# First product of the first MLP moved up to the transposes, and one attention unit started one tile later

## The chip, the cores and the metric

The kernel runs on one core of one Trainium2 chip. The metric is the device time of one execution in microseconds. Several executions of the same program are timed, and their median counts. One more execution is recorded by the hardware profiler; all rows below come from it.

## The reference

Three stages follow each other: a causal sparse attention, then two MLPs over its 2304 tokens.

```python
B, H, S, D = 4, 8, 576, 64
rel = pos[:, None] - pos[None, :]
mask_local   = (rel >= 0) & (rel < 32)                        # heads 0 to 3
mask_strided = (rel >= 0) & (pos[None, :] % 32 == pos[:, None] % 32)   # heads 4 to 7
attn = softmax(where(mask, q @ k.T / sqrt(D), -1e9)) @ v
x = attn.transpose(0, 2, 1, 3).reshape(2304, 512)             # tokens x (heads * D)
g = s * relu(x @ w_in) ** 2 + b                               # w_in 512 x 2048
y = g @ w_out                                                 # w_out 2048 x 512
out = ((y @ w_a) * (y @ w_b)) @ w_o2                          # w_a, w_b 512 x 1536
```

## The kernel before

**Numbers.** Every weight and activation that TensorE multiplies in the MLPs is split in two float32r halves, a high one made by ScalarE (ACT) and a low one made by VectorE (DVE) as source minus high. A product is then three matmuls, high by high, high by low, low by high (`PASSES`). The weights arrive as 64-bit floats; before the split each tile of 128 x 512 takes one ACT instruction (`raw`, a scaling) and three DVE instructions (a shift and two shift-and-or) to become float32.

**Blocks.** The first MLP runs over five token blocks. Block 0 holds the first 128 tokens of each of the four batches: 512 columns, of which the columns of batch bb are one quarter. Blocks 1 to 4 hold the rest of one batch each. A block is a loop over 16 tiles `f` of the 2048 hidden units. `h_mm(n, f)` makes one tile of h from x with 12 matmuls (four chunks `kk` of 128 of the 512 model dimensions, three passes each) into the one bank of the pool `ps_h`, then relu and square and the two halves of g. `o_mm` adds that tile's part of the output with 12 matmuls; it runs two tiles behind, so that the order of a tile is h(f), o(f-2), and then what `attend` issues.

**Opening.** x of block 0 comes from a dense little attention over the first 128 tokens of each batch (class `First`), whose order over all engines is written out in the string `ORDER`. Its last steps are `X` (TensorE transposes the result of one batch into a bank `fpx`), `hi` (ACT writes the high half of x for that batch's 128 columns and all four chunks `kk` at once) and `lo` (DVE writes the low half likewise). `I8` issues eight matmuls over constant data into a spare bank (`lull`). ACT's and DVE's instructions in `ORDER` are chained in that order.

**Attention beside the MLP.** x of block n+1 is made while the MLP of block n runs. A unit is a generator of steps for two heads: `local` for a window of 32 keys, `strided` for the strided heads. `plan(n)` puts each step behind a numbered tile, and `attend(number)` issues the steps of that tile, local units before strided ones. `in_order` makes every matmul of a step follow the last matmul issued before it, so TensorE's order is that of the code; within a step the planner may reorder matmuls that write different banks, but not those that add to one bank. ACT's and DVE's order is chosen by the planner when an instruction becomes ready; once queued, an instruction holds its place.

A local unit of block 1 has seven steps: (1) load q and k; (2) transpose them on TensorE (`pst`, two banks) and copy them by ACT into `qkT`; (3) load v, make the mask and the scores (`pss`, two banks), and DVE takes the row maximum; (4) four exponentials on ACT; (5) DVE normalises; (6) transpose the probabilities (`ppt`) and copy them by ACT into `pT`; (7) multiply with v (`po`) and write the halves of x. The first unit, u0, has its steps at (-5, -3, 0, 1, 1, 2, 3); a negative number is issued ahead of tile 0. The second, u1, has them at (1, 3, 4, 4, 5, 6, 7). The first strided unit, s0, has its transposes at 2 (three banks `pst`), its scores at 3 (two banks `pss`, into which no mask is multiplied: DVE adds it while it copies each bank out) and its exponentials at 4.

**Shared buffers.** The pool `ps_a` has three banks for all `pst`, `pss`, `ppt`, `po` of these units. `qkT` and `pT` of the local units share the one buffer of the tag `lT`. q and k of the local units share one buffer (`qk`), v another (`vn`). The exponentials of u0 are held behind the relu of the last tile of h issued before them.

Of the kernel before, what the change touches and what calls it, by code (L numbers as in the profile page):

```python
# [25 lines left out]
def sparse_attention_two_mlps(  # L26
# [21 lines left out]
    KD = DM // P  # L48
# [44 lines left out]
    def mm(*args, **kwargs):  # L93
        last_pe[:] = [nc.tensor.matmul(*args, **kwargs).ins]  # L94
# [15 lines left out]
    def split(hi, lo, src):  # L110
        nc.scalar.activation(out=hi, in_=src, func=AF.Copy)  # L111
        return nc.vector.tensor_tensor(out=lo, in0=src, in1=hi.bitcast(F32), op=ALU.subtract)  # L112
# [651 lines left out]
    def h_mm(n, f):  # L764
        T = T1[n]
        pool, tag = (ps_a, "a") if (n, f) == (0, 1) else (ps_h, "h")
        ph = pool.tile([P, TM], F32, tag=tag, name="h")[:, 0:T]
        m = 0
        for kk in (0, 2, 3, 1) if n and f == 0 else range(KD):
            for a, c in PASSES:  # L770
                mm(
                    ph, lhsT=wi[f][:, a, kk, :], rhs=x_t[n][:, c, kk, 0:T],
                    start=(m == 0), stop=(m == 3 * KD - 1),
                )
                m += 1
        with tc.high_priority(offset=URGENT):
            r = hp.tile([P, TM], F32, tag="r", name="r")[:, 0:T]
            relu = nc.scalar.activation(out=r, in_=ph, func=AF.Relu)  # L778
            gt = gp.tile([P, 2, TM], F32R, tag="gt", name="gt")
            hi, lo = gt[:, 0, 0:T], gt[:, 1, 0:T]  # L780
            if n == 0:
                nc.scalar.activation(out=r, in_=r, func=AF.Square)
                last = split(hi, lo, r)
            else:
                nc.scalar.activation(out=hi, in_=r, func=AF.Square)  # L785
                if n == 1:
                    nc.scalar.activation(out=gt[:, :, T:T + 2], in_=bc, func=AF.Copy)
                nc.vector.tensor_tensor(out=r, in0=r, in1=r, op=ALU.mult)  # L788
                last = nc.vector.tensor_tensor(out=lo, in0=r, in1=hi.bitcast(F32), op=ALU.subtract)  # L789
        behind[:] = [relu.ins, last.ins]  # L790
        return gt
# [212 lines left out]
    def plan(n):  # L1004
        at_n = (-2, 0, 1, 1, 2, 3, 4) if n == 1 else (-3, 0, 1, 2, 3, 4)
        at_f = (-3, 0, 1, 2, 4, 5) if n == 1 else (-3, 0, 1, 2, 3, 5)
        near = [
            (
                4 * i - 1,
                local(0, n, i % 2, TF + i // 2 * 4 * QT, 4 - i // 2) if n == 1  # L1010
                else local_pairs(n - 1, n, i % 2, TF + i // 2 * 8 * QS, 8 - i // 2 * 2),
                at_n,
            )
            for i in range(4)
        ]
        far = [(8 * i + 1, (strided if n == 1 else strided_pairs)(n - 1, n, i), at_f) for i in range(2)]
        if n == 1:
            near[0] = (0, near[0][1], (-5, -3, 0, 1, 1, 2, 3))
            far[0] = (1, far[0][1], (-5, 1, 2, 3, 5, 7))
        if n == 2:  # L1020
            near[0] = (-1, near[0][1], (-2, 0, 1, 2, 3, 4))
        for first_, gen, at in near + far:
            for t in at:
                steps.setdefault((n - 1) * NF1 + first_ + t, []).append(gen)
# [25 lines left out]
    def next_weights(number):  # L1050
# [13 lines left out]
    )  # L1064

    m_b = first_mask()
# [38 lines left out]
    for n in range(1, NB):  # L1105
        plan(n)
# [3 lines left out]
    for n in range(NB):  # L1110
# [11 lines left out]
        for f in range(NF1):  # L1122
            order = ExitStack()
            if n == 0:
                supply(len(wi) + len(wo) + 6)
                with after(behind + (last_w if f == 1 else []) or last_act + last_dve):
                    next_weights(min(1 if f == 0 else 2, len(order1) - len(wi) - len(wo)))
                order.enter_context(after(last_act + last_dve))
            gt = in_order(h_mm, n, f)
            queue.append((acc, gt, f, n))  # L1130
            if len(queue) > AHEAD1:
# [207 lines left out]
```

## Time and profile before

| what | value |
|---|---|
| time, median of 3 runs | 899.72 us (899.67 to 899.81) |
| the profiled execution's own time | 899.66 us |
| its span, first to last instruction | 897.6 us |
| TensorE matmuls (PE) busy | 888.7 us, 99% |
| TensorE weight loads (PEld) busy | 793.9 us, 88% |
| DVE busy | 621.8 us, 69% |
| ACT busy | 401.9 us, 45% |
| granted TensorE clock over the span | 1.000 |

The span is 2.06 us shorter than the time of the same execution. Matmuls are pipelined and their ends are modelled, so a PE that is busy 99% of the span is not yet one that never waits. A weight load (LDWEIGHTS) stands ahead of each matmul on the same engine, and a wait shows best as idle time ahead of a weight load: [0.95 <-ACT qkT L294] behind a row says that the engine stood idle for 0.95 us ahead of it, until that instruction of ACT released it.

### The profile page before, as it was taken

The numbers are of one execution on the slowest core, as the hardware profiler recorded it, in microseconds if no ns is written. First come the engines' busy times: TensorE is split into PE (matmuls) and PEld (weight loads), VectorE is DVE, ScalarE is ACT, GpSimd is POOL, SyncE is SP. The second block draws the span as 40 slices with busy tenths as digits, with TensorE's granted clock in tenths as the row PEclk, the third lists the DMA queues.
The fourth block names the chain that finished last, engine by engine and source line by source line (L and its number), as shares of the span: only waits on it lengthen the run. The fifth ranks groups of instructions, "written<-read, shape, count | busy, mean of one in ns | idle before, by whom it ended". The sixth has DMA issues, their size and how long they took to land.

```text
span 897.6 us, 16349 instructions
## 1 busy us (share of the span) xinstructions
PE 888.7 (99%) x6166; PEld 793.9 (88%) x6166; DVE 621.8 (69%) x1266; ACT 401.9 (45%) x866; POOL 42.0 (5%) x120
## 2 busy tenths in 40 slices
PE   8999999999999999999999999999999999999998
PEld 6778889999888899998889999988999988999986
DVE  6898995676766777727655777765676765776742
ACT  6777774434433353343333445444334444333322
POOL 6000000000000010000100000000000000000000
PEclk9999999999999999999999999999999999999999
DMA  9965534656665766446566443323432231333010
GB/s 232 283 209 161 166 78 133 164 143 166 201 168 163 178 190 169 133 130 225 195 198 225 131 141 112 131 87 108 148 99 98 89 94 59 124 95 106 30 36 35
DMA packets 156606, 126.41 MB, mean 141 GB/s; under 512 B 102256, under 2 KB 131440, under 8 KB 156528
## 3 DMA queue, kind: packets, MB, share of 16 engines
q1 hardware_dynamic: 149840, 109.12, 43.0%
q0 software_dynamic: 4608, 15.73, 4.5%
q8 instruction: 48, 0.79, 0.4%
q10 hardware_dynamic: 2080, 0.52, 0.3%
q14 instruction: 30, 0.25, 0.1%
HBM read 100.17 MB, written 25.17 MB: 140 GB/s over the span
## 4 chain that ended last, share of the span: by engine, by line
PE 96%; ACT 2%; DVE 1%; DMA 1%; issue 0%; SPq 0%; ACTq 0%
PE acc L94 38%; PE pp L94 29%; PE h L94 22%; PE po L94 2%; PE pss L94 1%; PE ppt L97 1%; PE fpo L94 1%; DMA fqk<-in_q_dram 1%; ACT raw L130 0%; ACT fpt L596 0%; PE fss L94 0%; PE fps L97 0%; PE pst L97 0%; PE fpp L97 0%; PE fpx L97 0%; ACT r L778 0%
## 5 line engine op out<-in xcount | busy, mean ns | idle before, releaser
L94 PE MATMUL pp<-x2w,wf 128*128 128x384 f32 x1512 | 265.8, 335 | 0.0
L94 PEld LDWEIGHTS pp<-x2w,wf 128*128 128x128 f32 x1512 | 263.0, 188 | 1.8 <-ACT u L596 0.4
L94 PE MATMUL h<-x,w 128*128 128x512 f32 (+1 forms) x960 | 217.1, 374 | 0.0
L94 PE MATMUL acc<-gt,w 128*128 128x512 f32 (+2 forms) x960 | 210.7, 368 | 1.0 <-ACT w L111 1.0
L94 PEld LDWEIGHTS acc<-gt,w 128*128 128x128 f32 x960 | 175.5, 188 | 24.0 <-ACT w L111 1.4
L94 PEld LDWEIGHTS h<-x,w 128*128 128x128 f32 x960 | 171.8, 188 | 24.3 <-DVE w L112 0.5
L94 PE MATMUL acc<-o2w,abt 128*128 128x512 f32 x648 | 150.5, 390 | 0.0
L94 PEld LDWEIGHTS acc<-o2w,abt 128*128 128x128 f32 x648 | 121.4, 188 | 24.6
L778 ACT ACTIVATE r<-h 128x512 f32<-128x512 f32 (+1 forms) x80 | 44.4, 555 | 156.3 <-PE h L94 152.6
L788 DVE TENSOR_TENSOR r<-r 128x384 f32<-128x384 f32 (+1 forms) x64 | 40.0, 625 | 91.8 <-ACT gt L785 91.6
L601 DVE TENSOR_TENSOR u<-pp,u 128x384 f32<-128x384 f32 x72 | 40.0, 555 | 64.8 <-PE pp L94 59.3
L596 ACT ACTIVATE u<-pp 128x384 f32<-128x384 f32 x36 | 17.8, 493 | 115.6 <-PE pp L94 115.6
L596 ACT ACTIVATE wf<-w2t 128x512 fp32r<-128x512 f32 x72 | 45.2, 628 | 21.2 <-PE pp L94 20.3
L601 DVE TENSOR_TENSOR wf<-w2t,wf 128x512 fp32r<-128x512 f32 x72 | 49.4, 686 | 0.3 <-ACT wf L596 0.3
L136 DVE SCALAR_TENSOR_TENSOR raw<-raw 128x512 uint32<-128x512 uint32 x66 | 44.4, 688 | 0.7
L130 ACT ACTIVATE raw<-raw 128x512 f32<-128x512 f32 x66 | 42.7, 672 | 2.9 <-DMA raw<-in_moe_w_a_dram 2.5
L789 DVE TENSOR_TENSOR gt<-r,gt 128x384 fp32r<-128x384 f32 (+1 forms) x64 | 40.0, 624 | 3.6
L601 DVE TENSOR_TENSOR wf<-w2r,wf 128x512 fp32r<-128x512 f32 x72 | 39.6, 550 | 0.0
L596 ACT ACTIVATE wf<-w2r 128x512 fp32r<-128x512 f32 x72 | 37.3, 518 | 4.5 <-PE pp L94 4.0
L601 DVE TENSOR_TENSOR abt<-dly,abt 128x384 fp32r<-128x384 f32 x36 | 19.9, 556 | 25.0 <-ACT abt L596 24.9
L596 ACT ACTIVATE abt<-c 128x384 fp32r<-128x384 f32 x36 | 18.8, 523 | 40.4 <-DVE c L601 40.4
L785 ACT ACTIVATE gt<-r 128x384 fp32r<-128x384 f32 (+1 forms) x64 | 36.5, 571 | 0.4
(150 smaller groups left out, 805.6 us busy)
## 6 DMA issues: line engine op xcount, KB each, us to landing
w2t<-w2s SPq DMA_DIRECT2D x36, 512.0 KB
w2r<-w2d SPq DMA_DIRECT2D x60, 256.0 KB
raw<-in_moe_w_out_dram SPq DMA_DIRECT2D x28, 512.0 KB
w2d<-w2s POOLq DMA_DIRECT2D x36, 256.0 KB, 3.3
raw<-in_moe_w_in_dram SPq DMA_DIRECT2D x16, 512.0 KB
raw<-in_moe_w_a_dram SPq DMA_DIRECT2D x12, 512.0 KB
raw<-in_moe_w_b_dram SPq DMA_DIRECT2D x12, 512.0 KB
w2s<-w2t POOLq DMA_DIRECT2D x12, 512.0 KB, 4.4
```

The lines of the kernel that those rows point to most:

```text
L94: last_pe[:] = [nc.tensor.matmul(*args, **kwargs).ins]
L97: last_pe[:] = [nc.tensor.transpose(*args).ins]
L130: nc.scalar.activation(out=high.bitcast(F32), in_=high.bitcast(F32), func=AF.Copy, scale=HIGH_SCALE)
L136: nc.vector.scalar_tensor_tensor(out=low, in0=high, scalar=3, in1=low, op0=ALU.logical_shift_left, op1=ALU.bitwise_or)
L596: i = nc.scalar.activation(**kwargs).ins
L601: i = getattr(nc.vector, method)(**kwargs).ins
L778: relu = nc.scalar.activation(out=r, in_=ph, func=AF.Relu)
L785: nc.scalar.activation(out=hi, in_=r, func=AF.Square)
L788: nc.vector.tensor_tensor(out=r, in0=r, in1=r, op=ALU.mult)
L789: last = nc.vector.tensor_tensor(out=lo, in0=r, in1=hi.bitcast(F32), op=ALU.subtract)
```

## The change

Three edits. `h_mm` takes the chunks of the first tile of block 0 in the order 0, 1, 3, 2. The steps (2) to (7) of u0 each move one tile later, step (2) from ahead of tile 0 to behind tile 0's h; its loads stay where they are. The eight `lull` matmuls behind the last `X` go, so that on TensorE the first h comes directly behind the transposes of x.

```diff
@@ h_mm @@
-        for kk in (0, 2, 3, 1) if n and f == 0 else range(KD):
+        for kk in range(KD) if f else (0, 2, 3, 1) if n else (0, 1, 3, 2):
             for a, c in PASSES:
                 mm(
                     ph, lhsT=wi[f][:, a, kk, :], rhs=x_t[n][:, c, kk, 0:T],
@@ plan @@
         if n == 1:
-            near[0] = (0, near[0][1], (-5, -3, 0, 1, 1, 2, 3))
+            near[0] = (0, near[0][1], (-5, 0, 1, 2, 2, 3, 4))
             far[0] = (1, far[0][1], (-5, 1, 2, 3, 5, 7))
@@ ORDER @@
-        "hi0 hi1 rc3 no2 no3 cl0 X3 lo0 lo1 hi3 X2 hi2 I8 lo3 lo2 d11 d21 ch1 cl1"
+        "hi0 hi1 rc3 no2 no3 cl0 X3 lo0 lo1 hi3 X2 hi2 lo3 lo2 d11 d21 ch1 cl1"
```

## Rows read from the trace of the kernel before

**Rows 1.** Busy time by stage (microseconds, instructions), then clock, DMA share, GB/s.

```profile
31.99:62.24 30.25, 28.32 (x200) 21.65 (x199) 27.85 (x55) 24.07 (x53) 0.00 (x0) 1.00 0.84 257
62.24:480.00 417.76, 417.76 (x3561) 362.37 (x3558) 295.87 (x648) 186.57 (x412) 27.42 (x50) 1.00 0.59 167
```

**Rows 2.** Timeline of the opening: start, microseconds, instruction, [idle before <-releaser].

```profile
2.92 2.74 PE L94 MATMUL lull<-ident_b 128*128 128x384 bf16 x8 [2.92 <-DVE ident_b L561]
...
28.70 2.08 ACT L596 ACTIVATE x<-fpx 128x512 fp32r<-128x512 f32 x4 [2.25 <-PE fpx L97]
...
29.46 2.48 DVE L601 TENSOR_TENSOR x<-fpx,x 128x512 fp32r<-128x512 f32 x4
29.79 1.03 SPq L298 DMA_DIRECT2D vn<-in_v_dram  x2
...
29.93 1.46 PE L94 MATMUL lull<-ident_b 128*128 128x384 bf16 x8
...
31.07 0.61 PEld L97 LDWEIGHTS pst<-ident,qk 128*128 128x128 f32 x5
...
31.64 0.69 ACT L294 ACTIVATE qkT<-pst 128x256 f32<-128x256 f32 x2 [0.87 <-PE pst L97]
...
31.99 2.38 PEld L94 LDWEIGHTS h<-x,w 128*128 128x128 f32 x11 [0.18 <-DVE x L601]
32.01 0.37 SPq L283 DMA_DIRECT2D qk<-in_q_dram  x1
```

**Rows 3.** Timeline of TensorE's weight loads, 33 to 63 us.

```profile
35.40 2.60 PEld L94 LDWEIGHTS h<-x,w 128*128 128x128 f32 x12
...
39.12 2.15 PEld L94 LDWEIGHTS h<-x,w 128*128 128x128 f32 x10 [0.47 <-DVE w L112]
42.72 2.61 PEld L94 LDWEIGHTS acc<-gt,w 128*128 128x128 f32 x12 [1.45 <-ACT w L111]
45.37 0.58 PEld L97 LDWEIGHTS ppt<-ident,lpt 128*96 128x96 f32 x4
...
47.22 2.60 PEld L94 LDWEIGHTS h<-x,w 128*128 128x128 f32 x12
49.85 2.68 PEld L94 LDWEIGHTS acc<-gt,w 128*128 128x128 f32 x12
52.88 0.55 PEld L94 LDWEIGHTS po<-pT,vn 96*64 96x64 f32 x16 [0.35 <-issue]
53.50 0.50 PEld L97 LDWEIGHTS pst<-ident,qk 128*128 128x128 f32 x5
54.95 0.88 PEld L94 LDWEIGHTS pss<-sqkT 64*64 64x64 f32 x32 [0.95 <-ACT qkT L294]
55.91 2.58 PEld L94 LDWEIGHTS h<-x,w 128*128 128x128 f32 x12
58.53 2.68 PEld L94 LDWEIGHTS acc<-gt,w 128*128 128x128 f32 x12
61.47 0.12 PEld L94 LDWEIGHTS <-ident_b 128*128 128x128 bf16 x2 [0.26 <-issue]
...
62.24 0.76 PEld L94 LDWEIGHTS h<-x,w 128*128 128x128 f32 x4
```

**Rows 4.** Timeline of ACT, 28 to 63 us.

```profile
39.05 0.34 ACT L237 ACTIVATE lpt<-pss,mx 128x96 f32<-128x96 f32 x1
...
40.32 1.28 ACT L130 ACTIVATE raw<-raw 128x512 f32<-128x512 f32 x2
...
41.97 0.69 ACT L111 ACTIVATE w<-raw 128x512 fp32r<-128x512 f32 x1
...
46.36 0.58 ACT L319 ACTIVATE pT<-ppt 96x512 f32<-96x512 f32 x1
```

**Rows 5.** Timeline of DVE, 28 to 63 us.

```profile
35.73 0.61 DVE L231 TENSOR_REDUCE mx<-pss 128x2 f32<-128x192 f32 x2
...
57.28 0.82 DVE L243 TENSOR_TENSOR spt<-pss,smask 128x288 f32<-128x288 f32 x2
```

## The prediction

> **What bounds the kernel now.** I read the busy times by stage first, since they say how far a delay travels. From 62.24 us to 480 us TensorE has a matmul under way in all of the 417.76 us, while from 31.99 to 62.24 it has one in 28.32 of 30.25 us [rows 1]. 62.24 is where h of tile 5 starts, the first work behind the last step that the change moves (u0's step 7, now behind tile 4). So I take what h(5) gains or loses as what the whole time gains or loses, and look only at the 30 us ahead of it.
>
> Next I read what opens that stretch. ACT's four high halves of x end at 28.70 + 2.08 = 30.78, DVE's four low halves at 29.46 + 2.48 = 31.94, and the weight load of h(0)'s second matmul starts at 31.99, named as released by DVE [rows 2]. DVE's last low half sets the start of h(0), not TensorE, which fills the time before with the eight `lull` matmuls and u0's transposes.
>
> Then the weight loads from 33 to 63 us, for the waits between the tiles [rows 3]. The reader is to see four. h(2) has its last ten loads at 39.12 though h(1)'s ended at 38.00: less two loads at 0.22 us each, 0.7 us of idling for weight halves. o(0) waits 1.45 us for ACT's half of its weights. At tile 3 the strided scores wait 0.95 us for ACT to empty u1's banks. At tile 4 there is only the 0.26 us that each such group of scores pays for issue. Between 31.99 and 62.24 DVE is busy 27.85 us and ACT 24.07 us [rows 1], so the weight halves of the first tiles are bound by these two, DVE before ACT.
>
> **The change part by part.**
>
> *Order of chunks, and the place of h(0).* Each `hi` and `lo` writes one batch's 128 columns of all four chunks; each product of h reads all 512 columns of one chunk. So any chunk needs all four quarters, and the order 0, 1, 3, 2 releases nothing. All twelve products add to one bank and keep their order; the second reads low halves. Only the first product can move, to about 30.85. The second still loads at 31.99, and h(0) ends its loads at 34.37 as before. The 1.46 us of `lull` and the 0.61 us of transposes that leave [rows 2] lay under DVE's low halves: gain 0. If that cover were not there, the most to be had would be 31.99 - 30.85 = 1.1 us.
>
> *The transposes behind h(0).* They now cost TensorE their 0.61 us in the open [rows 2], and the scores leave this place: those took 34.37 to 35.40, 1.03 us [rows 2, 3]. h(1) starts at 34.98, 0.4 us earlier, and ends its loads at 37.6. The scores behind it end at 38.6, inside the time in which h(2) waited for weights. So on TensorE both are free up to h(2).
>
> *ACT and DVE up to o(0).* u0's two copies took 0.69 us at 31.64, where ACT had idled 0.87 us [rows 2]. Now they stand behind h(0)'s relu, where ACT scales weights and makes the halves of g one after another, and DVE's next weights wait for those. Bounds 0 and 0.69; I take 0.69, for I see no idle time there. DVE's two row maxima, 0.61 us [rows 5], move from 35.73 to about 38.7, into the same chain: 0 to 0.61, I take 0.3. The other way, the exponentials leave ACT's queue ahead of o(0)'s weights, 39.05 to 40.32, 1.27 us; those weights come at 41.97 [rows 4]. That is worth 0 to 1.27; DVE being the fuller of the two, I take 0.3. Sum: o(0) at 42.72 + 0.7 = 43.4.
>
> *Tile 2.* u0's `ppt`, 0.58 us, leaves; s0's transposes, 45.95 to 47.22 = 1.27 us [rows 3], stay. They need three banks, two of which hold u0's scores until the exponentials, now behind h(2)'s relu, are done. o(0)'s 2.61 us covers most of that; uncovered 0 to 1.27, taken 0.2, since the scalings came only behind the exponentials (40.32 behind 39.05 [rows 4]) and so won't hold them up. h(3): 43.4 + 2.61 + 1.27 + 0.2 = 47.5, 0.3 late. ACT then carries the exponentials and not the 0.58 us copy of `pT` [rows 4], 0.69 us more, ahead of o(1)'s weights; o(1) followed h(3) at 49.85 without a wait [rows 3]. 0 to 0.69, taken 0.2. I stand at +0.5.
>
> *Tile 3.* Here the shared buffer tells. u0 now writes `pT` at this tile and reads it at the next; u1's copies into `qkT` want the same buffer `lT`, so they wait, and with them u1's two `pst` banks stay full. s0's two score banks must be had one after the other out of the third bank: `ppt` 0.58, its end 0.15, ACT's copy 0.58 and 0.2 until ACT is free, half of the scores' 0.88, DVE's mask add 0.41, the other 0.44, releases 0.2, all [rows 3 to 5] but the small ones. How long DVE lets the add wait: before, it came at 57.28 though the score loads ended at 55.83, 1.45 us later; nobody waited for it. 0 to 1.45, I take 0.7. Sum 3.7 us, against 52.53 to 55.91 = 3.38. I stand at +0.8; bounds of this tile -0.4 and +1.1.
>
> *Tile 4.* Before, 61.21 to 62.24, 1.03 us. Now u0's product with v, 0.35 + 0.55 [rows 3]; then u1's copies, 0.69 as at 31.64 [rows 2], with 0.1 to start and 0.2 for ACT to come free; then u1's scores, 0.77 without the issue gap. 2.66 us, +1.6; bounds +1.3 (ACT free at once) and +2.4 (a weight half and a half of x ahead of the copies, 0.69 and 0.39). Nothing else is on TensorE between, by the order of the code.
>
> *DMAs.* u0's loads of q and k stay. Its loads of v (1.03 us of SP's queue) come a tile later for a use a tile later. u1's q and k, first issued at 32.01 [rows 2], now wait for u0's transposes, to 35.0 in place of 31.7, with weight loads behind them on SP's queue. The use is at 53.50, and the weights run six tiles of 128 x 512 ahead: 0, for up to 3.3 us of waiting. POOL has no part.
>
> *Sum.* 0.7 + (0.3 - 0.7) + 0.2 + 0.3 + 1.6 = **+2.4 us**. The profiled execution took 899.66 us, 0.06 under the median, so 902.1 us. All low ends together give about -1, all high ends about +6.
>
> One queue matters for tile 4. Between h(1)'s relu and its square ACT ran four exponentials and two scalings, from 39.05 to 41.6 [rows 4]: what is queued goes first. [...]
>
> **The rivals.**
>
> *The exponentials give it back (not slower).* Place: ACT ahead of o(0). If ACT and not DVE set o(0)'s 41.97, the 1.27 us comes off in full and h(2)'s wait is already filled. Then o(0) is at 42.72 + 0.69 + 0.3 - 1.27 = 42.44, 1.0 us better than in my sum, and tiles 3 and 4 at their low ends take 1.0 less: 902.1 - 2.0 = 900.1 us. It decides if tiles 3 and 4 cost under 1.8 us more than o(0) gains. For it speaks o(0)'s wait, released by ACT [rows 3]; against it DVE's 27.85 of 30.25 us.
>
> *h(0) does go by quarters.* If products that need only high halves went first, eight would fit between 30.85 and 32.6, and h(0) would end 0.9 us earlier, and relu and all weights with it: 901.2 us. Against it: in [rows 2] the loads stop at the second product.
>
> *ACT is held up at tile 4.* The copies are queued ahead of h(4)'s relu or the halves for tile 5, and all of it waits for u0's product: 2 us more, 904.1 us. The planner queues what it takes to be ready, and its times are not the chip's.
>
> *The clock falls.* Without `lull`, TensorE has one product between 30.0 and 31.99. After the opening's idle 2.92 us eight such matmuls took 2.74 us, and 1.46 later [rows 2]. At that pace h(0) and h(1) would take 88% more, 2 x 2.6 x 0.88 = 4.6 us: 906.7. [...]
>
> **How the numbers follow.** Forecast 0.58, exponentials 0.22, quarters 0.05, ACT held up 0.12, clock 0.03. A measurement of this kernel tells 0.2%, 1.8 us, from no change. Of the forecast, a sixth lies under +1.8; of the exponentials' case nearly all lies within 1.8 us, some 0.03 below. Faster 0.03, same 0.31, slower 0.66. A tenth on either side leaves 900.0 to 904.6 us; the forecast's own range is 901.0 to 903.6.
>
> **What would show it.** Right: the load of h(0)'s second product still at about 32.0, idle TensorE before it, clock 1.00; u0's copies behind h(0)'s relu; o(0) at 43 to 44; the strided scores of tile 3 in two groups with a wait for DVE between; u1's scores at tile 4 waiting some 0.8 us or more for ACT `qkT`; h(5) at 64 to 65 and no waits after. Wrong: h(0) ending before 34, o(0) before 42.7, or u1's scores at tile 4 following `po` at once.

## The result, and the profile after

The changed kernel took 905.51 us (median of 6 runs, 903.60 to 906.78), the kernel before 899.74 in the same comparison (6 runs, 899.50 to 899.81): a ratio of 1.0064, 95% interval 1.0051 to 1.0077, so 5.8 us slower. 902.1 was forecast, with a range up to 904.6: the sign was right, the loss more than twice as large. The profiled execution took 905.85 us, with a span of 903.8 and a mean granted clock of 0.998 (before: 899.66, 897.6, 1.000). The runs of one kernel now differ by 3 us, where those of before differed by 0.3. Two single executions in the comparisons further down, one of 2257 us (order and lull alone) and one of 3107 us (the kernel before), are left out of every median and range.

Where the time went is read by setting equal weight loads of the two traces side by side:

| place | before | after | behind by |
|---|---|---|---|
| h(0), second product | 31.99 | 32.61 | 0.62 |
| h(5) | 62.24 | 65.30 | 3.06 |
| h behind `po` of block 1's tile 7 | 194.29 | 198.89 | 4.60 |
| the next h | 199.46 | 205.63 | 6.17 |
| span | 897.6 | 903.8 | 6.2 |

The first 0.62 us come before anything that the change touches (at 7.5 us a transpose waits 0.58 us for a load where it waited 0.29, and the transposes of x start 0.63 us late); over the kernels below it is anything from -0.1 to 0.6, so I take it off. What is left is 2.44 us up to h(5), nothing for 130 us, and then 3.1 us in a place where the change moves nothing.

The busy times by stage, as in [rows 1] (columns as there). The first row has 32.69 us where it had 30.25; in the second TensorE is no longer busy throughout: 1.37 us are idle.

```profile
32.61:65.30 32.69, 28.74 (x204) 22.63 (x204) 28.62 (x57) 25.59 (x54) 0.00 (x0) 1.00 0.73 225
65.30:480.00 414.70, 413.33 (x3533) 358.86 (x3530) 293.23 (x643) 183.16 (x407) 27.36 (x50) 1.00 0.60 166
```

The opening, against [rows 2]. DVE's four low halves of x end at 32.56, and the second product loads right behind them; ahead of it TensorE idles. That is as before, without the `lull`.

```profile
29.32 2.08 ACT L596 ACTIVATE x<-fpx 128x512 fp32r<-128x512 f32 x4 [2.25 <-PE fpx L97]
...
30.08 2.48 DVE L601 TENSOR_TENSOR x<-fpx,x 128x512 fp32r<-128x512 f32 x4
...
31.45 0.19 PEld L94 LDWEIGHTS h<-x,w 128*128 128x128 f32 x1 [0.98 <-ACT x L596]
```

TensorE's weight loads of the first tiles, against [rows 3]. h(2) no longer waits, o(0) waits longer, and the strided scores of tile 3 come in two groups of 16 with 1.50 us of DVE between them. At tile 4 `po` is followed by u1's scores only 1.70 us later.

```profile
32.61 2.40 PEld L94 LDWEIGHTS h<-x,w 128*128 128x128 f32 x11 [0.97 <-DVE x L601]
35.05 0.67 PEld L97 LDWEIGHTS pst<-ident,qk 128*128 128x128 f32 x5
...
39.29 2.61 PEld L94 LDWEIGHTS h<-x,w 128*128 128x128 f32 x12
44.12 2.61 PEld L94 LDWEIGHTS acc<-gt,w 128*128 128x128 f32 x12 [2.22 <-ACT w L111]
...
50.49 2.68 PEld L94 LDWEIGHTS acc<-gt,w 128*128 128x128 f32 x12
...
54.73 0.57 PEld L94 LDWEIGHTS pss<-sqkT 64*64 64x64 f32 x16 [0.40 <-ACT pT L319]
56.79 0.57 PEld L94 LDWEIGHTS pss<-sqkT 64*64 64x64 f32 x16 [1.50 <-DVE spt L243]
57.44 2.60 PEld L94 LDWEIGHTS h<-x,w 128*128 128x128 f32 x12
60.08 2.68 PEld L94 LDWEIGHTS acc<-gt,w 128*128 128x128 f32 x12
63.11 0.55 PEld L94 LDWEIGHTS po<-pT,vn 96*64 96x64 f32 x16 [0.35 <-issue]
...
64.81 0.37 PEld L94 LDWEIGHTS pss<-qkT 64*64 64x64 f32 x16 [0.37 <-issue]
65.30 2.61 PEld L94 LDWEIGHTS h<-x,w 128*128 128x128 f32 x12
```

Now block 1's tile 7. First the kernel before, from the timelines of SP's queue, ACT and the weight loads. The load of a piece of the second MLP's `w_a` is issued at 183.85, ACT waits 1.21 us for it, and nothing reaches TensorE.

```profile
183.85 0.39 SPq L118 DMA_DIRECT2D raw<-in_moe_w_a_dram  x1
188.09 0.69 ACT L130 ACTIVATE raw<-raw 128x512 f32<-128x512 f32 x1 [1.21 <-DMA raw<-in_moe_w_a_dram]
193.70 0.54 PEld L94 LDWEIGHTS po<-pT,vn 64*64 64x64 f32 x24 [0.25 <-issue]
194.29 2.04 PEld L94 LDWEIGHTS h<-x,w 128*128 128x128 f32 x12
```

The changed kernel, same views and DVE. The load is issued at 190.33, 3.4 us later than 183.85 + 3.06. ACT stands 4.82 us at its first instruction on the piece, with the square of h and the copy of `pT` queued behind it; DVE waits 5.57 us for that square; DVE's mask add, queued behind all this, frees the score bank that `po` needs, so TensorE stands 1.48 us (the matmuls of `po` behind the first four).

```profile
190.33 0.39 SPq L118 DMA_DIRECT2D raw<-in_moe_w_a_dram  x1
194.73 0.68 ACT L130 ACTIVATE raw<-raw 128x512 f32<-128x512 f32 x1 [4.82 <-DMA raw<-in_moe_w_a_dram]
195.85 0.56 DVE L788 TENSOR_TENSOR r<-r 128x384 f32<-128x384 f32 x1 [5.57 <-ACT gt L785]
198.06 0.51 DVE L419 TENSOR_TENSOR sqk<-pss,smask 128x144 f32<-128x144 f32 x2
198.41 0.44 PEld L94 LDWEIGHTS po<-pT,vn 64*64 64x64 f32 x20 [1.48 <-DVE sqk L419]
198.89 2.95 PEld L94 LDWEIGHTS h<-x,w 128*128 128x128 f32 x12
```

That wait is the first 1.5 us. The second is the clock, in the column behind POOL's (busy times of TensorE, its loads, DVE, ACT, POOL, then the granted clock): right behind the wait it is 0.50, and from this h to the next it takes 6.7 us where it took 5.2 before.

```profile
198.00:200.00 2.00, 1.59 (x26) 1.54 (x27) 1.97 (x6) 0.00 (x0) 0.05 (x1) 0.96 0.00 0
200.00:202.00 2.00, 2.00 (x8) 2.00 (x7) 1.49 (x5) 1.23 (x5) 0.49 (x1) 0.50 0.48 61
202.00:204.00 2.00, 2.00 (x10) 2.00 (x9) 1.12 (x6) 1.46 (x3) 0.00 (x0) 0.68 0.91 352
```

So the questions for the chip are: is the 2.44 us the shared buffer `lT`; why does a load 130 us later come late; and when does the clock fall?

### The profile page after: what moved, and what is told of

Same layout as the page of the kernel before. It is cut to its first block, busy times and chain, and to the rows that moved or that the text cites. A ratio compares the mean times of both kernels' runs of the same rounds, so it can differ in the third digit from the quotient of the medians.

```text
span 903.8 us, 16335 instructions
## 1 busy us (share of the span) xinstructions
PE 890.0 (98%) x6158; PEld 795.7 (88%) x6158; DVE 621.7 (69%) x1266; ACT 401.0 (44%) x866; POOL 41.9 (5%) x120
## 4 chain that ended last, share of the span: by engine, by line
PE 93%; DVE 3%; ACT 2%; DMA 1%; issue 0%; SPq 0%; DVEq 0%; ACTq 0%
PE acc L94 37%; PE pp L94 29%; PE h L94 21%; PE po L94 2%; PE pss L94 1%; PE ppt L97 1%; PE fpo L94 1%; DMA fqk<-in_q_dram 1%; DVE raw L136 1%; ACT fpt L596 1%; DMA raw<-in_moe_w_a_dram 0%; DVE w L112 0%; DVE raw L133 0%; DVE raw L140 0%; ACT raw L130 0%
```

## The experiments

Twelve kernels ran, each compared with the kernel before, whose medians in these comparisons lie between 899.59 and 899.62 us. "h(5)" is its start less the 62.24 of before, and less the opening's offset (that of h(0)'s second product), so that it compares with 2.44. Where h(0)'s products are sorted, the second product no longer marks the opening, and h(5) is given without that.

**The parts by themselves.** First the order and the lull alone, u0 at its old place:

```diff
-        for kk in (0, 2, 3, 1) if n and f == 0 else range(KD):
+        for kk in range(KD) if f else (0, 2, 3, 1) if n else (0, 1, 3, 2):
-        ... X3 lo0 lo1 hi3 X2 hi2 I8 lo3 lo2 ...
+        ... X3 lo0 lo1 hi3 X2 hi2 lo3 lo2 ...
```

> The kernel before without the eight lull matmuls and with the chunk order 0, 1, 3, 2; u0 and its transposes stay ahead of h(0). Theory 1 (the lull lay under the low halves of x, the order of chunks releases nothing): h(0) starts and ends where it did, h(5) within 0.3 us of the 62.24 of before (less what the opening differs), time 899.7 +- 0.5 us, granted clock 1.000. Rival (the clock falls without the lull): h(0) and h(1) up to 88% longer, up to 904.3 us, clock below 1.000 around 31 to 37 us. Rival (the quarters release h(0) earlier): h(0) ends up to 1.1 us earlier, 898.6 us.

Measured: 900.60 us (899.51 to 903.80 over 10 runs), ratio 1.0012 (1.0003 to 1.0022). h(5) is at +0.04 us, so neither order nor lull counts in the first tiles: theory 1 holds there, both rivals fall. But the runs scatter over 4 us, and the profiled one, of 903.80, has the whole second loss: `po` of block 1's tile 7 waits 1.98 us, and 3.64 us are gone behind it. SP's order of loads is that of the kernel before. So the second loss does not come from the shift of u0.

```profile
196.41 0.64 PEld L94 LDWEIGHTS po<-pT,vn 64*64 64x64 f32 x20 [1.98 <-DVE sqk L419]
```

Then the shift alone:

```diff
-            near[0] = (0, near[0][1], (-5, -3, 0, 1, 1, 2, 3))
+            near[0] = (0, near[0][1], (-5, 0, 1, 2, 2, 3, 4))
```

> The kernel before with u0's steps a tile later alone; the lull and the old order of chunks stay. Theory 1 (the shift is the whole loss, in two places): h(5) about 2.4 us late, the strided scores of tile 3 in two groups, u1's scores at tile 4 behind the product with v; and, since SP's queue then has the order that it has in the changed kernel, the second loss of about 3.1 us at block 1's tile 7 as well: 904 to 906 us. If the second loss hangs on something else than SP's order: 902.1 us. Rival (leaving out the lull is what costs): within 0.5 us of 899.7.

Measured: 903.37 us (902.45 to 904.73), ratio 1.0042 (1.0030 to 1.0054). h(5) is +2.39: the first loss is the shift's. The profiled execution, the fastest, has no wait at tile 7, although SP's order is that of the changed kernel. This part of theory 1 falls for that execution: there the second loss belongs to the *other* part of the change, the one that costs nothing where it stands. The four other runs are 0.8 to 2.3 us longer at clocks of 0.995 to 0.998, and none of them was profiled; the kernels below decide for them too.

```profile
196.17 0.55 PEld L94 LDWEIGHTS po<-pT,vn 64*64 64x64 f32 x24 [0.25 <-issue]
```

**A buffer of its own for the local units' `qkT`,** in the changed kernel:

```diff
-        qkT = lp.tile([P, 9 * QT], F32, tag="lT", name="qkT")
+        qkT = lp.tile([P, 9 * QT], F32, tag="lQ", name="qkT")
```

> The changed kernel with a buffer of its own for the local units' qkT (tag lQ in place of lT), so that u1's copies need not wait for u0's product with v. Theory 1 (the shared buffer makes tiles 3 and 4 late): the strided scores of tile 3 follow one another in one group or with under 0.5 us of wait, u1's scores of tile 4 wait under 0.2 us, h(5) 1.5 to 2.0 us earlier than in the changed kernel, that is 0.4 to 0.9 us behind the kernel before; whether the second loss at block 1's tile 7 comes depends on the loads there: 900.3 us without it, 903.5 with it. Rival (ACT and DVE, with more to do in each tile, set tiles 3 and 4): h(5) within 0.5 us of the changed kernel's, 905 us.

Measured: 900.97 us (899.35 to 904.58 over 12 runs), ratio 1.0017 (1.0005 to 1.0029). h(5) is at -0.22: the first loss is gone altogether, a little more than expected. The two rows that it touches (weight loads) are one group of 32 strided scores, and u1's scores 0.88 us behind `po`:

```profile
54.48 0.88 PEld L94 LDWEIGHTS pss<-sqkT 64*64 64x64 f32 x32 [0.40 <-ACT pT L319]
...
61.08 0.55 PEld L94 LDWEIGHTS po<-pT,vn 96*64 96x64 f32 x16 [0.35 <-ACT r L782]
...
61.96 0.37 PEld L94 LDWEIGHTS pss<-qkT 64*64 64x64 f32 x16 [0.16 <-issue]
```

The scatter stays, and the profiled run, of 903.32, loses 3.3 us at block 1's tile 7.

**The loads of the second MLP's weights on POOL's queue,** behind the stores of converted weights, in the changed kernel:

```diff
-                words[i] = stage((w_a, w_b, w_o2)[kind], f, kind < 2, raw)[0]
+                words[i] = stage((w_a, w_b, w_o2)[kind], f, kind < 2, raw, nc.gpsimd)[0]
```

> The changed kernel with the loads of the second block of weights (w_a, w_b, w_out of the second MLP) issued on POOL's queue in place of SP's, nothing else. Theory 1 (at block 1's tile 7 the load of w_a, late on SP's queue, holds up ACT, DVE and then TensorE): h(5) stays 2.4 us late, no matmul waits over 1 us from there to the end of block 1, granted clock 1.000, about 902.3 us. Rival (the stall is made by the order of ACT's and DVE's work, or by TensorE's own order, not by the load): the stall of 1.5 us and the clock's fall stay, 905 us.

Measured: 904.29 us (903.50 to 904.82), ratio 1.0049 (1.0037 to 1.0061). The wait at tile 7 is gone, as theory 1 said: from h(5) to 480 us only 0.3 us are lost. The time missed it all the same. In the profiled execution that is because the clock fell at another place, behind tile 3's wait of 1.48 us, and h(5) is +3.87 in place of +2.44. The slices of the profiled execution:

```profile
56.00:58.00 2.00, 1.31 (x17) 1.16 (x18) 2.00 (x5) 0.00 (x0) 0.00 (x0) 0.69 0.56 113
58.00:60.00 2.00, 2.00 (x5) 1.61 (x6) 2.00 (x5) 0.56 (x1) 0.00 (x0) 0.50 0.98 349
```

**Why the lull counts 130 us later.** The traces of these kernels were compared around 163 us, where the late load has its root. At tile 3 of block 1 two transfers become free at once when DVE has converted a piece: POOL's store of the result (256 KB) and SP's next load of `w_a` (512 KB). In the kernel before, one packet on the queue of instructions falls between 162.5 and 163.0 us, and SP's issue of the load then lasts 1.38 us where others last 0.39 (DMA queues of that half microsecond: packets, MB, share of 16 engines; then SP's timeline):

```profile
q8 instruction: 1, 0.02, 12.0%
```

```profile
162.93 1.38 SPq L118 DMA_DIRECT2D raw<-in_moe_w_a_dram  x1
```

In the order-only kernel the packet falls between 164.5 and 165.0, behind both, and lasts 0.299 x 16 x 0.5 = 2.4 us in place of 0.96. The load is issued 0.06 us ahead of the store, in 0.44 us; the store lands after 6.3 us in place of 3.1; DVE waits 2.38 us for it with the next conversion, and the next load of `w_a` is issued 2.7 us late (187.04), and ACT can start on it only at 192.75 (the same two views, then DVE's timeline):

```profile
q8 instruction: 1, 0.02, 29.9%
```

```profile
163.44 0.44 SPq L118 DMA_DIRECT2D raw<-in_moe_w_a_dram  x1
163.50 0.54 POOL L825 DMA_DIRECT2D w2d<-w2s  x1 [9.76 <-DVE w2s L140]
...
169.83 0.69 DVE L140 SCALAR_TENSOR_TENSOR w2s<-raw 128x512 uint32<-128x512 uint32 x1 [2.38 <-DMA w2d<-w2s]
```

In the changed kernel the packet falls between 167.0 and 167.5, 164.2 when its 3.06 us are taken off, lasts 1.9 us, and the load is issued 0.19 us behind the store, which lands after 4.9 us.

The profile of the changed kernel counts 48 such packets over the span (q8 instruction, 0.79 MB), and 6,158 matmuls of TensorE and as many weight loads: 257 instructions to a packet, so I take them for fetches of TensorE's own instructions. That is an estimate from these counts; the views name the queue, not whose instructions they are. The eight `lull` matmuls are 16 instructions with their weight loads; at block 1's pace (24 in 2.04 us) that is 1.4 us, and the packet moved by about as much: from 162.89 to 164.54 in the order-only kernel, 1.2 us when the offset of 0.5 is taken off, and 1.3 us in the changed kernel. So I put the 16 instructions back at a place where they cost nothing, o(0)'s wait, in the order-only kernel:

```diff
             gt = in_order(h_mm, n, f)
+            if (n, f) == (0, 2):
+                lull = acc[3][:, 0:3 * P]
+                in_order(idle, 8)
```

> The order-only kernel (no lull ahead of h(0), u0 at its old place) with the same eight matmuls put back between h(2) and o(0), where TensorE idles 1.45 us and more; they write a bank that o(0) overwrites. It tells why leaving out the lull let block 1's tile 7 stall. Theory (the 16 instructions themselves matter: without them the 16 KB transfer on the instruction queue falls about 2 us later, behind the load of w_a and not ahead of it, and w_a then overtakes the store of converted weights): the transfer falls at 162 us again, no wait over 1 us at tile 7 of block 1, 899.4 to 900.0 us with all runs under 900.6, clock 1.000. Rival (the lull keeps TensorE's clock or the opening's timing, by being ahead of h(0)): scatter and stall stay as in the order-only kernel, 899.5 to 903.8 us, median about 900.9. Were the eight matmuls not hidden, +1.3 us on either.

Measured: 899.62 us, 11 runs from 899.51 to 900.30, ratio 1.0000 (0.9992 to 1.0009). The scatter is gone, `po` of tile 7 waits 0.25 us, and the packet is back between 162.5 and 163.0, 1.3 us long. SP stands 1.83 us at the transfer ahead, and the load of `w_a` comes 1.3 us behind the store, which lands after 2.7 us (timelines of SP, POOL and the weight loads):

```profile
162.65 1.83 SPq L267 DMA_DIRECT2D sqk<-in_k_dram  x1
...
163.30 0.54 POOL L825 DMA_DIRECT2D w2d<-w2s  x1 [9.77 <-DVE w2s L140]
...
164.60 0.52 SPq L118 DMA_DIRECT2D raw<-in_moe_w_a_dram  x1
...
193.96 0.54 PEld L94 LDWEIGHTS po<-pT,vn 64*64 64x64 f32 x24 [0.25 <-issue]
```

The next load of `w_a` is still 2.0 us late here (186.10) and ACT waits 2.77 us for it, but tile 7 hides that much; it did not hide 2.7 us. The traces of all ten kernels, above and below, that load on SP's queue agree. In the seven with the 16 instructions the packet starts 0.1 to 0.9 us behind the start of DVE's conversion, the store lands after 2.6 to 3.1 us, and tile 7 has no wait. In the three without them it starts 2.0 to 2.2 us behind, the store lands after 4.9 to 6.7 us, and tile 7 waits 1.48 to 1.98 us.

**Both cures, and the lull at its old place.** In the changed kernel, own buffer and POOL's queue together:

> The changed kernel with both cures: a buffer of its own for the local units' qkT, and the loads of the second MLP's weights on POOL's queue, behind the stores of converted weights. Theory (two losses, one of 2.4 us at tiles 3 and 4 from the shared buffer, one of about 3 us at block 1's tile 7 from a load that overtakes a store; the clock falls only behind such stalls): h(5) within 0.4 us of before, no wait over 1 us at tile 7, clock 1.000 in all runs, 899.2 to 900.0 us, all runs within 1 us of each other. Rival (without the lull the clock falls by itself): clock below 0.999 in some runs and a median of 901 or more.

Measured: 900.12 us (899.35 to 901.52), ratio 1.0008 (0.9999 to 1.0017). h(5) is -0.24 and tile 7 has no wait, but the runs spread over 2.2 us, and the four above 900.7 have a clock of 0.997 to 0.998. Neither theory: both losses are cured, and something still lets the clock fall in some runs.

The same with the lull kept, own buffer, all loads on SP's queue and the old order of chunks (the shift of u0 and the tag, from the kernel before):

> The kernel before with u0's steps a tile later and the buffer of its own, the lull and the old chunk order kept, all loads on SP's queue. Theory (shared buffer for the first loss; the instructions of the lull for the second): h(5) within 0.4 us of before, no stall at tile 7, clock 1.000 in all runs, 899.0 to 899.8 us with a spread under 1 us. Rival (the second loss comes from the shift of u0 and SP's order, not from the lull's instructions): scatter up to 904 us and a median near 901, as with the own buffer without the lull.

Measured: 901.03 us, ratio 1.0011 (1.0002 to 1.0019), and its 11 runs are of two kinds: four from 899.57 to 899.90 at a clock of 0.999 to 1.000, seven from 900.96 to 901.26 at 0.997 to 0.998. The profiled one is of the second kind, and shows the place. o(0) waits 2.24 us for ACT, the clock reads 0.64 and then 0.51 behind it, and o(0)'s loads take 4.18 us in place of 2.61 (a row of weight loads, then the slices):

```profile
43.40 4.18 PEld L94 LDWEIGHTS acc<-gt,w 128*128 128x128 f32 x12 [2.24 <-ACT w L111]
```

```profile
41.00:43.00 2.00, 0.59 (x3) 0.16 (x1) 2.00 (x6) 1.76 (x4) 0.00 (x0) 1.00 1.02 376
43.00:45.00 2.00, 1.60 (x4) 1.31 (x5) 2.00 (x5) 2.00 (x7) 0.00 (x0) 0.64 1.06 378
45.00:47.00 2.00, 2.00 (x6) 1.51 (x6) 2.00 (x6) 2.00 (x9) 0.00 (x0) 0.51 0.81 167
```

h(5) is at +1.43 by it. Tile 7 has no wait (`po` 0.25 us), with u0 shifted and SP's order the changed kernel's but for a few loads that move some places: the 16 instructions decide it, at either place. And the clock falls with the lull in place, so it is not the lull ahead of h(0) that holds it up; it falls behind the wait of o(0), which the shift of u0 lengthens from 1.45 [rows 3] to 2.2 us. That the six other runs of this kind fall at the same place is likely from their times and was not profiled.

**The eight matmuls in o(0)'s wait,** in the changed kernel (edit as above), alone:

> The changed kernel with nothing but the eight matmuls put back between h(2) and o(0), in o(0)'s wait of 2.2 us. Theory (three separate losses: 2.4 us at tiles 0 to 4 from the shared buffer and a fuller ACT and DVE; the stall at block 1's tile 7, because 16 instructions fewer move a fetch of instructions; the clock's fall, in some runs, behind each stall of 1.5 us and more): the first loss stays, the second goes, the clock can still fall behind the 1.5 us wait of tile 3: 902.0 us with runs up to 903.3. Rival (the second loss comes from the shift of u0 and SP's order): 904 to 906 us.

Measured: 902.61 us (902.02 to 903.68), ratio 1.0035 (1.0022 to 1.0048). It is 3.0 us behind the kernel before in place of 5.8, so 2.8 us are back. The first loss stays; the profiled run, of 903.48, has the clock's fall behind tile 3's wait of 1.50 us (h(4)'s loads take 4.17 us in place of 2.60, and the clock reads 0.50 from 58 to 60 us) and none elsewhere. With the buffer of its own as well:

> The changed kernel with the buffer of its own for qkT and the eight matmuls between h(2) and o(0). Theory: all three losses are cured, h(5) within 0.4 us of before, clock 1.000, 899.2 to 899.8 us, all runs within 1 us. Rival (the clock falls without the lull ahead of h(0), or the second loss belongs to SP's order): scatter to 901 and above as with the own buffer alone.

Measured: 899.46 us, 11 runs from 899.25 to 900.06, ratio 1.0000 (0.9991 to 1.0009); h(5) at -0.19, clock 0.999 or 1.000 in every run. o(0) now waits 0.85 us behind the eight matmuls. With the two edits the 5.8 us are gone, and the shift of u0 itself is worth nothing. The eight matmuls do two things here: they give back the 16 instructions, and they shorten o(0)'s wait; the kernel with the lull at its old place did the first alone, and its clock fell.

```profile
43.45 2.63 PEld L94 LDWEIGHTS acc<-gt,w 128*128 128x128 f32 x12 [0.85 <-ACT w L111]
```

**The race without the 16 instructions:** the order-only kernel with the loads on POOL's queue.

> The order-only kernel (no lull at all, u0 at its old place) with the loads of the second MLP's weights on POOL's queue behind the stores. It takes away the race of the w_a load and the store without giving the 16 instructions back. Theory (the fetch matters only because it decides that race): no wait over 1 us at block 1's tile 7, 899.4 to 900.2 us, all runs under 900.8. Rival (the fetch, or the lull, delays something else): stall and scatter to 903.8 stay.

Measured: 900.40 us (900.05 to 900.89 over 11 runs), ratio 1.0008 (1.0000 to 1.0017). Scatter and wait are gone without the instructions, so these matter only through the loads. But the store is still late: the load is issued 0.54 us behind it, it lands after 4.6 us, and DVE waits 1.58 us for it with the next conversion. What is gone is the place of the loads behind the others on SP's queue: the next load of `w_a` is issued at 184.28, where the kernel before had 183.85. The median lies 0.2 us over what was expected, and the highest run 0.1: at tile 3 of block 1 a transpose waits 0.77 us (rows of the timeline of POOL and DVE).

```profile
162.89 0.55 POOL L825 DMA_DIRECT2D w2d<-w2s  x1 [9.45 <-DVE w2s L140]
163.43 0.76 POOL L118 DMA_DIRECT2D raw<-in_moe_w_a_dram  x1
...
167.97 0.69 DVE L140 SCALAR_TENSOR_TENSOR w2s<-raw 128x512 uint32<-128x512 uint32 x1 [1.58 <-DMA w2d<-w2s]
```

**Halves in order.** The change is said to go quarter by quarter, which its order of chunks can't do. Sorting h(0)'s products does (with both cures, the lull left out; then with the own buffer and the eight matmuls in o(0)'s wait):

```diff
+        products = [(kk, a, c) for kk in ... for a, c in PASSES]
+        if (n, f) == (0, 0):
+            products.sort(key=lambda p: p[2])
```

> As the kernel with both cures, and h(0)'s twelve products sorted: first the eight that read x's high halves, then the four that read the low ones, so that h(0) need not wait for DVE's last low half after its first product. Theory of the prediction's second rival: eight products run between ACT's last high half and DVE's last low one, h(0) ends its loads 0.6 to 0.9 us earlier, and h(5) with it, if ACT's and DVE's work behind h(0)'s relu moves up as well: 898.6 to 899.0 us. Rival (the weights for h(2) and o(0) are set by DVE's own queue, full from the opening on): h(0) ends earlier, h(5) does not, as the kernel with both cures, within 0.2 us.

> As the changed kernel with the buffer of its own and the eight matmuls in o(0)'s wait, and h(0)'s products sorted, the eight that read x's high halves first. Theory (ACT and DVE set the tiles behind): h(0) ends its loads about 0.7 us earlier, o(0) 0.6 us earlier, h(5) under 0.3 us earlier; 898.9 to 899.6 us. Rival (h(0)'s end sets the chain): h(5) 0.7 us earlier, 898.6 us or less.

Measured: the first 900.73 us (899.38 to 901.85), ratio 1.0011 (1.0002 to 1.0020), where the clock falls behind o(0)'s wait of 2.34 us in the profiled run (0.997 over its span); the second 899.00 us (898.76 to 900.68), ratio 0.9995 (0.9986 to 1.0004), the fastest kernel here but within what can't be told from before. Its h(0) runs in one go, 12 loads from 31.05, and ends at 33.65 where the kernel without the sorting ended at 34.37; o(0) starts 0.23 us earlier, h(5) 0.25, although the opening is 0.2 us later. With that, h(0) gains 0.9 us and half of it reaches h(5); o(0) still waits 0.99 us for ACT, and neither theory has the size.

## Why the prediction was right, and where it failed

- *h(0) is held by DVE's last low half; order and lull gain nothing there.* Right: the second product loads at 32.61 - 0.62 = 31.99, and the order-only kernel has h(5) at +0.04.
- *o(0) at 43.4.* 44.12 - 0.62 = 43.50. Right.
- *Tile 2, standing at +0.5 at o(1).* 50.49 - 0.62 = 49.87, +0.02: half a microsecond too much.
- *Tile 3 at 3.7 us.* Two groups with DVE between, as drawn, but 57.44 - 53.17 = 4.27: DVE began the add 1.0 us after the first score loads ended (56.30 behind 55.30), where I took 0.7, and the rest of the 0.57 us is not explained. *Tile 4 at 2.66.* 65.30 - 62.76 = 2.54. The sum up to h(5) came to 2.44 against the forecast +2.4; that it is so near is luck, since half a microsecond too much at o(1) and 0.6 too little at tile 3 cancel. That the shared buffer makes it, the kernel with a buffer of its own shows: -0.22.
- **The step that failed** is the first, "I take what h(5) gains or loses as what the whole time gains or loses", with its two supports: the DMAs at 0 ("the weights run six tiles of 128 x 512 ahead") and "no waits after" h(5). The six tiles are the first MLP's weights. Those of the second MLP, whose loads compete with the stores (a store landed after 4.9 us with such a load 0.19 us behind it, after 2.7 us with 1.3 us between them), go through two buffers (`raw`, two deep), and nothing in the sum looked at them. They cost 1.5 us at tile 7 in the profiled run and 1.6 for the clock behind: 3.1 us of waits and clock that the sum put at 0.
- *The lull costs nothing to remove.* Right where it stands, wrong for the program: without the 16 instructions a packet on the queue of instructions came 1.2 us later at 163 us, and `po` of tile 7 waited 1.98 us (the order-only kernel). Putting them back in o(0)'s wait takes 2.8 us off the changed kernel.
- *The clock rival, at 906.7 us.* The time came near it, by another way. Its pace was that of the eight matmuls behind the opening's idle time, and in the kernel before the granted clock reads 1.00 there too, from 2.92 to 5.66 us, so that their 2.74 us are not shown to be the clock's. It did not fall without the lull at h(0) and h(1) (1.00 in [rows 1]'s first row and in the one after); it fell behind new waits of 1.48 to 2.34 us, in some runs, for 1.4 to 1.6 us each. *The exponentials give it back*: o(0) was 0.8 us late and not 0.3 us early as this rival had it; by o(1) the delay was gone, for a reason that no run here shows, and tiles 3 and 4 cost 2.4 us. *Quarters*: not with this order; with sorted products h(0) gained 0.9 us, as the rival had it, but only half of that reached h(5). *ACT held up at tile 4*: it was not, but at tile 7 by a load, in just that manner: one instruction at the head of ACT's queue waits 4.82 us, and the square of h and the copy of `pT` behind it.

## What to carry to other kernels

A stage in which TensorE is busy 100% can stand close to a wait that the busy time does not show, as here from 62.24 to 480 us: at block 1's tile 7 ACT waited 1.21 us for a load and TensorE not at all, and with ACT's 4.82 us TensorE stood 1.48. Look in such a stage for loads that arrive just in time and share an engine's queue with work on the path; here the order-only kernel's wait of 1.98 us at 196 us was gone with 16 instructions put back at 42 us. Time a changed kernel many times: here a spread of 3 us where there was 0.3 came with a race between two transfers and with falls of the clock. And price a buffer shared by two steps by its order of uses: here moving one user a step later made the other wait, for 2.44 us up to h(5), and a second buffer brought that to -0.22.

## What the runs showed of the hardware

- Taking out 16 TensorE instructions at 30 us moved a packet on the instruction queue at 163 us by 1.2 us (the order-only kernel), and with it whether a 512 KB load was issued beside a 256 KB store or behind it. SP's issue lasts 1.38 us (the kernel before) and 1.83 us (the eight matmuls put back) beside the packet, in place of 0.4 to 0.5; how the one makes the other stays open.
- The granted clock went to 0.50 behind single waits of 1.48 us (tile 3, the loads on POOL's queue) and 1.48 us (tile 7, the changed kernel) and to 0.51 behind one of 2.24 us (o(0), own buffer with the lull), and each fall cost 1.4 to 1.6 us. It did not in every run: the changed kernel's own waits of 2.22 us (o(0)) and 1.50 us (tile 3) left it at 1.00. What makes one run fall and the next not was not tried.
- The 256 KB store landed after 6.3 us where the 512 KB load was issued 0.06 us ahead of it, after 4.9 us with the load 0.19 us behind it, and after 2.7 us with the load 1.3 us behind.
